# Fourth to eighth tile: the first product of mm2 is issued ahead of mm1's last two block products

## The chip, the cores and the metric

One NeuronCore of a Trainium2 chip runs the kernel. It has five engines, each with its own instruction queue worked through in order: TensorE (PE, matrix products; its weight loads are shown apart, as PEld), VectorE (DVE), ScalarE (ACT), GpSimd (POOL) and SyncE (SP), which here issues almost all the DMAs. The metric is the device time of one execution in microseconds. Three timed runs of the kernel before gave 269.88, 270.17 and 270.53 us; the median is 270.17 us.

## What is computed

Chunked attention over 8 batches of 576 tokens with 8 heads of 64, then a two-layer network with exact GELU over all 4608 tokens. The reference, cut:

```python
# attention inside chunks of 64 keys
scores = scale * np.matmul(q_c, k_c.transpose(0, 1, 2, 4, 3))
attn = np.exp(scores - max) / sum
x = np.matmul(attn, v_c)                # then 4608 x 512
# network: w_in is 512 x 2048, w_out is 2048 x 512
h = x @ w_in
g = 0.5 * h * (1.0 + erf(h * inv_sqrt2))
return g @ w_out
```

## The kernel before

**Tiles.** There are nine tiles of 512 tokens: for each batch its first 512 tokens, and a ninth tile with the last 64 tokens of all eight. For each tile the kernel runs `mm1` (x times w_in, then GELU into `h`, bf16) and `mm2` (`h` times w_out, stored as `y`). The attention of the next tiles is slipped between the products of `mm2`. The schedule is the program's own: every engine takes its instructions in the order in which the Python emits them, and a semaphore wait is put in wherever one reads or overwrites what another has not finished.

**Seven products.** From the fourth tile on (t = 3 to 8) both layers use a Winograd form of the 2 x 2 block product: seven block products in place of eight, with sums of blocks formed by VectorE and running sums kept in PSUM banks. In `mm1` the 2048 features are cut into four groups a, b, c, d. A group's products are numbered 1 to 7, each of them four matmuls (`prod`, L677). Products 1 and 2 go to a bank X, 7 and 4 to a bank Z, and 6, 5 and 3 to a bank Y that starts as a copy of product 1.

**The order by words.** `mm1_groups` (L646) reads its order from a string, `FOUR` (L639) for the tiles of this change. "3b" is product 3 of group b. "c1a" is the ACT copy of X into Y (L714), "c2a" the ACT copy and "c3a" the DVE copy of Y's running sum into SBUF (L725), "a1a" and "a2a" are the DVE additions of Z to these (L728). "g12d" is the GELU on ACT (L684) of group d, first feature half, second token half; "g21d" has the second feature half and the first token half. "h1", "h2", "h3" are the DVE sums of blocks of `h` (`h_sums`, L576 and L577) over two, four and two of the eight feature blocks. The tail of `FOUR` is

```
2c g11d 5d a1c 7d c3d 3c g21b 4c g11c 3b a1d
g22c 4d g12c g12b 3d a2c a2d g21c g22d g12d g21d h2 h3
```

**mm2.** `mm2_seven` (L761) runs seven products of sixteen matmuls each. Here they are named in their order before:

1. the first product, bank X (L781), copied by ACT into bank Y (L782); then the attention of the next tile, called by `also(1)`: the activation table for Exp, `rows_av` (64 small matmuls, L347) and `rows_x` (DVE, L362 and L363, with two DMA transposes on SP, L366)
2. the S2 product, added to Y (L787), which ACT then copies to `s2` (L788)
3. the second product, added to X (L789); ACT copies it to `y` (L790), and SP stores that quarter of the output (L791, issued in L857)
4. the S1 product, added to the same Y (L792), copied by ACT to `s5` (L793)
5. the T4 product in bank Z (L796), with the scores of a later tile (`quad_S`, L247) in its middle
6. the S3 product in bank W (L800)
7. the S4 product, added to Y (L805)

The banks of `mm1`'s Y and those of `mm2` (X, Y, Z, W) come in turn from one pool of three, `ps_mm`. A bank that is taken again waits for the last reader of its earlier use. The ninth tile has its own `mm2`, `last_seven` (L810).

Of the kernel before, what the change touches and what calls it, by code (L numbers as in the profile page):

```python
# [11 lines left out]
def kernel(  # L12
# [10 lines left out]
    P = 128  # L23
    f32 = mybir.dt.float32
# [547 lines left out]
    def h_sums(t, j0, j1):  # L572

        a11, a12, a21, a22 = h_blocks(t, j0, j1)
        s1, s2 = h_sum(t, 1, j0, j1), h_sum(t, 2, j0, j1)
        nc.vector.tensor_tensor(s1, a21, a22, op=mybir.AluOpType.add)  # L576
        nc.vector.tensor_tensor(s2, s1, a11, op=mybir.AluOpType.subtract)  # L577
# [37 lines left out]
    def x_sums(t, which=(1, 3, 2, 4)):  # L615
# [7 lines left out]
        for i in which:  # L623
# [16 lines left out]
               g12a c1d 2b a2a g22b 6d 5c g21a a2b 2d 7c h1 g11b c3c c2d 2c g11d 5d a1c 7d c3d 3c g21b 4c g11c 3b a1d  # L640
               g22c 4d g12c g12b 3d a2c a2d g21c g22d g12d g21d h2 h3"""

    FOURS = range(FIRST7, NT)
    PROGRAMS = {1: LATE, 2: THIRD, **{t: FOUR for t in FOURS}}

    def mm1_groups(t, extra, between={}):  # L646

        st = tiles[t]
        st["h"] = hpool.tile([P, FF, MT], bf16, tag="h", name="h")
        h = st["h"][:].rearrange("p f (m e) -> p f m e", m=2)  # L650
        b11, b12, b21, b22 = x_blocks(t)
        w = in_blocks()
        TT, add = nc.vector.tensor_tensor, mybir.AluOpType.add
        banks, sums = {}, {}
        four = t in FOURS
        tags = {"a": ("y_1", "y_2"), "b": ("y_5", "rc" if four else "y_2"), "d": ("y_1", "rc")}
        first = {"a": 0, "b": 4, "c": 2, "d": 6}
        plain = [] if four else [j + FH * r for j in (6, 7) for r in range(2)]
        hs = {"h1": (0, 2), "h2": (2, 6), "h3": (6, 8)}

        def prod(g, n):
            q, e = first[g] // 4, first[g] % 4
            if n in (1, 2):
                lhs, rhs, name = w[:, n - 1, :, 0, q, e:e + 2], b11 if n == 1 else b21, "X"
            elif n == 3:
                lhs, rhs, name = w_s[g, 4], b22, "Y"
            elif n == 4:
                lhs, rhs, name = w[:, 1, :, 1, q, e:e + 2], st["T"][4], "Z"
            else:
                lhs, rhs, name = w_s[g, n - 4], st["T"][n - 4], "Z" if n == 7 else "Y"  # L670
            fresh = n in (1, 7)
            if fresh:
                pool, tag = (ps_tp, "tp") if four and name == "Z" else (ps_at, "at")
                banks[g + name] = pool.tile([P, 2, TH], f32, tag=tag, name=f"h_{name}")
            for i in range(2):
                for kk in range(2):
                    nc.tensor.matmul(banks[g + name][:, i], lhs[:, kk, i], rhs[:, kk], start=fresh and i == kk == 0,  # L677
                                     stop=(kk == 1), skip_group_check=True)

        def gelu(g, r, m):  # L680
            j = first[g] + FH * r
            src = {(0, 0): lambda: banks[g + "X"], (0, 1): lambda: banks[g + "Y"],
                   (1, 0): lambda: sums[g, 0], (1, 1): lambda: sums[g, 1]}[r, m]()
            nc.scalar.activation(h[:, j:j + 2, m], src[:], Act.Gelu)  # L684

        for word in PROGRAMS.get(t, PROGRAM).split():
            for u in extra.pop(word, ()):
                u()
            if word == "start":
                begun = mm1_slot(t, [plain.pop(0) for _ in range(4)], between, 1)  # L690
            elif word == "sums":
                x_sums(t)
            elif word == "p" and t == 1:
                begun.pop()()
            elif word == "p":
                f = plain.pop(0)
                bank = ps_tp.tile([P, MT], f32, tag="tp", name="h_ps")
                for ks in range(KS):
                    nc.tensor.matmul(bank[:].rearrange("p (s e) -> p s e", s=2), w_in_sb[:, ks, f * P:(f + 1) * P],  # L699
                                     by_halves(t)[:, :, ks] if t >= FIRSTX else  # L700
                                     st["x"][:, ks, :].rearrange("p (s e) -> p s e", s=2),
                                     start=(ks == 0), stop=(ks == KS - 1))
                nc.scalar.activation(st["h"][:, f, :], bank[:], Act.Gelu)
            elif word in hs:
                if t >= FIRST7:
                    h_sums(t, *hs[word])
            elif word[0].isdigit():
                prod(word[1], int(word[0]))
            elif word[0] == "g":
                gelu(word[3], int(word[1]) - 1, int(word[2]) - 1)  # L710
            elif word[:2] == "c1":
                g = word[2]
                banks[g + "Y"] = ps_mm.tile([P, 2, TH], f32, tag="mm", name="h_Y")
                AC(banks[g + "Y"][:], banks[g + "X"][:])  # L714
            elif word[:2] in ("c2", "c3"):
                g, i = word[2], int(word[1]) - 2
                if g != "c":
                    tag = tags[g][i]
                    sums[g, i] = work.tile([P, 2, TH], f32, tag=tag, name=f"h_{g}", bufs=2 if tag == "rc" else 1)
                elif i == 0:  # L720
                    pool, tag = (hsum, "s3") if t < B else (ypool, "y")
                    pair = pool.tile([P, 4, TH], f32, tag=tag, name="h_sb")
                    sums[g, 0] = pair[:, 0:2]
                    sums[g, 1] = pair[:, 2:4]
                (AC if i == 0 else DV)(sums[g, i][:], banks[g + "Y"][:])  # L725
            elif word[0] == "a":
                g, i = word[2], 2 - int(word[1])
                TT(sums[g, i][:], banks[g + "Z"][:], sums[g, i][:], op=add)  # L728
# [13 lines left out]
    def product(out, lhs, rhs, fresh, behind=lambda m: None, ms=range(TH // P)):  # L742

        for m in ms:
            for f in range(FH):
                nc.tensor.matmul(out[m], lhs[:, f, m * P:(m + 1) * P], rhs[:, f, :],  # L746
                                 start=fresh and f == 0 and (m == 0 or len(out) == 3), stop=(f == FH - 1),
                                 skip_group_check=True)
            behind(m)
# [8 lines left out]
    def halves(bank):  # L758
        return [bank[:, 0], bank[:, 1]]

    def mm2_seven(t, at={}):  # L761

        def also(i):
            for u in at.get(i, ()):
                u()
        st = tiles[t]
        h = st["h"][:].rearrange("p (k f) (m e) -> p k f m e", k=2, m=2)
        w = w_out_sb[:].rearrange("p (k f) (n e) -> p k f n e", k=2, n=2)
        T = [None] + [w_t[i] for i in range(1, 5)]
        def bank_mm():  # L770
            return ps_mm.tile([P, 2, NH], f32, tag="mm", name="y_ps")
        X, Y = bank_mm(), bank_mm()
        s2, s5 = (work.tile([P, 2, NH], f32, tag=nm, name=nm, bufs=1) for nm in ("y_2", "y_5"))
        y = [ypool.tile([P, 2, d_model], f32, tag="y", name="y_sb") for _ in range(2)]
        TT, add = nc.vector.tensor_tensor, mybir.AluOpType.add
        if t == B:
            s1 = work.tile([P, 2, NH], f32, tag="y_1", name="y_1", bufs=1)
            last_seven(t, h, w, T, (X, Y, bank_mm()), (s1, s2, s5), y)
            return
        also(0)  # L780
        product(halves(X), h[:, 0, :, 0], w[:, 0, :, 0], True)  # L781
        AC(Y[:], X[:])  # L782
        Z = bank_mm()
        st["Z"] = Z[:].rearrange("p m n -> p (m n)")
        also(1)
        h_third(t)
        product_by_f(halves(Y), h_sum(t, 2), T[2])  # L787
        AC(s2[:], Y[:])  # L788
        product(halves(X), h[:, 1, :, 0], w[:, 1, :, 0], False)  # L789
        AC(y[0][:, :, :NH], X[:])  # L790
        store(t, 0, 0, y)  # L791
        product(halves(Y), h_sum(t, 1), T[1], False)  # L792
        AC(s5[:], Y[:])  # L793
        h_fourth(t)
        also(2)
        product(halves(Z), h[:, 1, :, 1], T[4], True, lambda m: also((2, m)))  # L796
        TT(s2[:], Z[:], s2[:], op=add)
        also(3)
        W = bank_mm()
        product(halves(W), h_sum(t, 3), T[3], True)  # L800
        TT(y[1][:, :, NH:], W[:], s5[:], op=add)
        TT(y[1][:, :, :NH], W[:], s2[:], op=add)
        store_whole(t, 1, y)
        also(4)
        product(halves(Y), h_sum(t, 4), w[:, 1, :, 1], False)  # L805
        AC(y[0][:, :, NH:], Y[:])
        store(t, 0, 1, y)
        also(5)
# [406 lines left out]
```

## Time and profile before

| | us |
|---|---|
| median of three timed runs | 270.17 |
| the profiled execution, whole | 270.41 |
| its span, first to last instruction | 268.6 |
| PE busy in the span | 259.6 (97%) |
| DVE busy | 202.1 (75%) |
| ACT busy | 187.1 (70%) |
| POOL busy | 77.0 (29%) |

The profile shows one execution. In the timeline each row has the start in us from the span's start, the length in us, the engine, the line of the kernel, the operation, output and inputs, and how many instructions are merged; a bracket at the end has the idle time of the engine ahead of it and what ended it. A matmul's row lasts longer than the time until the next matmul may start, since matmuls are pipelined: sixteen of 256 columns take 1.75 us from start to start of what follows, and the row shows 1.91. The fifth tile (t = 4) is the one followed below; its `mm2` begins at 147.05 us.

### The profile page before, as it was taken

How to read it: one execution, taken by the hardware profiler on the slowest of the kernel's cores; microseconds unless marked ns; L12 is line 12 of the kernel's file. 1: busy time of each engine (PE TensorE's matmuls, PEld its weight loads, DVE VectorE, ACT ScalarE, POOL GpSimd, SP SyncE). 2: the span in 40 equal slices, each digit the busy share in tenths (PEclk: the TensorE clock that was granted, in tenths of full speed). 3: DMA queues.
4: the chain of work that ended last, by engine and by line, in shares of the span. 5: the costliest groups of instructions: out<-in, count | busy, mean ns of one | idle time of the engine just before them, and what ended most of it. 6: DMA issues, size and time to landing. Idle time of an engine off the chain costs nothing.

```text
span 268.6 us, 7554 instructions
## 1 busy us (share of the span) xinstructions
PE 259.6 (97%) x3077; PEld 195.6 (73%) x3092; DVE 202.1 (75%) x372; ACT 187.1 (70%) x364; POOL 77.0 (29%) x130
## 2 busy tenths in 40 slices
PE   7989999999999999999999999999999999999993
PEld 3554454476548654888888888888888888888882
DVE  2565775989997879589569956995699769958961
ACT  3466756797767967897689669957995799239700
POOL 3735667361440061441044103500362030000000
PEclk9999999999999999999999999999999999999998
DMA  7999999997979959999899989988886760430005
GB/s 230 285 377 402 395 388 243 237 286 194 336 205 261 244 123 231 279 237 191 232 232 231 177 216 242 264 152 206 237 193 146 166 192 0 89 138 12 2 2 156
DMA packets 127075, 56.59 MB, mean 211 GB/s; under 512 B 103488, under 2 KB 120896, under 8 KB 127040
## 3 DMA queue, kind: packets, MB, share of 16 engines
q1 hardware_dynamic: 126592, 55.59, 79.4%
q10 hardware_dynamic: 448, 0.52, 0.7%
q8 instruction: 24, 0.39, 0.6%
q14 instruction: 11, 0.09, 0.1%
HBM read 36.70 MB, written 9.44 MB: 172 GB/s over the span
## 4 chain that ended last, share of the span: by engine, by line
PE 92%; ACT 2%; DVE 1%; DMA 1%; issue 1%; POOL 0%; SPq 0%; ACTq 0%; DVEq 0%; POOLq 0%
PE y_ps L746 24%; PE h_Y L677 15%; PE y_ps L866 12%; PE h_Z L677 10%; PE h_X L677 10%; PE h_ps L538 6%; PE y_ps L891 4%; PE y_ps L755 4%; PE s_ps L247 2%; PE h_ps L699 1%; DMA arrival<-in_k_dram 1%; PE tp L170 1%; ACT y_ps L782 1%; PE warm L958 1%; PE rc_ps L484 1%
## 5 line engine op out<-in xcount | busy, mean ns | idle before, releaser
L677 PEld LDWEIGHTS <-w_in_s 128*128 128x128 bf16 x480 | 46.8, 98 | 6.1
L677 PEld LDWEIGHTS <-w_in_sb 128*128 128x128 bf16 x360 | 35.1, 98 | 6.5
L677 PE MATMUL h_X<-x,w_in_sb 128*128 128x256 bf16 x240 | 33.7, 272 | 0.0
L677 PE MATMUL h_Y<-x_t,w_in_s 128*128 128x256 bf16 x240 | 32.7, 272 | 0.0
L866 PE MATMUL y_ps<-w_out_sb,h 128*128 128x512 bf16 x137 | 31.7, 379 | 0.9 <-issue 0.8
L746 PEld LDWEIGHTS <-h_s 128*128 128x128 bf16 x304 | 29.7, 98 | 3.6 <-issue 0.2
L746 PEld LDWEIGHTS <-h 128*128 128x128 bf16 x288 | 27.8, 98 | 3.4
L218 POOL CAST v_nat<-arrival 128x1024 bf16<-128x1024 f32 x14 | 14.8, 1061 | 48.4 <-DMA arrival<-in_v_dram 48.3
L164 POOL CAST q_nat<-arrival 128x512 bf16<-128x512 f32 x33 | 19.4, 627 | 28.2 <-DMA arrival<-in_q_dram 19.1
L164 POOL CAST k_nat<-arrival 128x512 bf16<-128x512 f32 x34 | 21.9, 678 | 14.0 <-DMA arrival<-in_k_dram 10.1
L746 PE MATMUL y_ps<-w_t,h_s 128*128 128x256 bf16 x208 | 24.8, 273 | 0.0
L866 PEld LDWEIGHTS <-h 128*128 128x128 bf16 x144 | 13.3, 98 | 15.0 <-issue 0.2
L746 PE MATMUL y_ps<-w_out_sb,h 128*128 128x256 bf16 x192 | 22.9, 273 | 0.0
L963 ACT ACT_TABLE_LOAD x16 | 20.5, 1283 | 1.0 <-PEq L1199 0.7
L684 ACT ACTIVATE h<-h_Y 128x512 bf16<-128x512 f32 x30 | 17.7, 595 | 2.4 <-PE h_Y L677 1.9
L714 ACT COPY h_Y<-h_X 128x512 f32<-128x512 f32 x30 | 17.0, 582 | 2.8 <-PE h_X L677 2.6
L684 ACT ACTIVATE h<-h_X 128x512 bf16<-128x512 f32 x30 | 17.8, 597 | 1.4 <-PE h_X L677 0.6
L677 PE MATMUL h_Z<-x_t,w_in_s 128*128 128x256 bf16 x120 | 18.0, 273 | 0.0
L677 PE MATMUL h_Y<-x,w_in_s 128*128 128x256 bf16 x120 | 17.7, 273 | 0.0
L677 PE MATMUL h_Z<-x_t,w_in_sb 128*128 128x256 bf16 x120 | 17.4, 272 | 0.0
L725 DVE COPY h_a<-h_Y 128x512 f32<-128x512 f32 x8 | 5.5, 692 | 14.1 <-PE h_Y L677 14.1
L254 ACT ACTIVATE pT<-s_ps 128x512 bf16<-128x512 f32 x28 | 14.5, 601 | 2.3 <-PE s_ps L247 2.3
(148 smaller groups left out, 489.4 us busy)
## 6 DMA issues: line engine op xcount, KB each, us to landing
arrival<-in_q_dram SPq DMA_DIRECT2D x7, 1024.0 KB
arrival<-in_k_dram SPq DMA_DIRECT2D x24, 256.0 KB
out_dram<-y_sb SPq DMA_DIRECT2D x23, 256.0 KB
arrival<-in_v_dram SPq DMA_DIRECT2D x20, 256.0 KB
arrival<-in_moe_w_out_dram SPq DMA_DIRECT2D x4, 1024.0 KB
arrival<-in_v_dram SPq DMA_DIRECT2D x30, 128.0 KB
out_dram<-y_sb SPq DMA_DIRECT2D x5, 512.0 KB
arrival<-in_moe_w_in_dram SPq DMA_DIRECT2D x4, 512.0 KB
```

The source lines that it names most:

```text
L164: copy(st[nm][:, g].rearrange("p j r d -> p r j d"), st[nm + "f"][:, 2 * g:2 * g + 2])
L218: copy(st["v"][:, part[0], part[1], :D], st["vf"][:, part[0], part[1]])
L254: nc.scalar.activation(pT[:].rearrange("p u (c j) -> p u c j", j=J), s_ps[g2][c][:].rearrange("p u (j c) -> p u c j", j=J), Act.Exp, scale ...
L538: nc.tensor.matmul(h_ps[a][:], w_in_sb[:, ks, f * P:(f + 1) * P], st["x"][:, ks, :], start=(ks == 0), stop=(ks == KS - 1))
L677: nc.tensor.matmul(banks[g + name][:, i], lhs[:, kk, i], rhs[:, kk], start=fresh and i == kk == 0, stop=(kk == 1), skip_group_check=True)
L684: nc.scalar.activation(h[:, j:j + 2, m], src[:], Act.Gelu)
L714: AC(banks[g + "Y"][:], banks[g + "X"][:])
L746: nc.tensor.matmul(out[m], lhs[:, f, m * P:(m + 1) * P], rhs[:, f, :], start=fresh and f == 0 and (m == 0 or len(out) == 3), stop=(f == FH ...
L755: nc.tensor.matmul(out[m], lhs[:, f, m * P:(m + 1) * P], rhs[:, f, :], start=False, stop=(f == FH - 1), skip_group_check=True)
L866: nc.tensor.matmul(y_ps[:], st["h"][:, f, ms * P:(ms + 1) * P], w_out_sb[:, f, :], start=(f == 0), stop=(f == FF - 1))
L891: nc.tensor.matmul(tiles[t]["y_ps", ms][:], tiles[t]["h"][:, f, ms * P:(ms + 1) * P], w_out_sb[:, f, :], start=(f == 0), stop=False)
L963: nc.scalar.activation(act_scratch[:], rest[:, 0:1], func)
```

## The change

Tiles t = 3 to 7 take their order in `mm1` from a new string, `AHEAD`; the ninth keeps `FOUR`. In `AHEAD` two words are new: "X" issues the first product of `mm2`, and "cX" takes bank Y and issues its ACT copy. "X" stands behind 4c and ahead of 4d and 3d. 3b has moved from behind 4c to ahead of 3c, "h2" stands ahead of a2d, and some GELUs have changed places. `mm2` then begins with the second product, by feature blocks (`product_by_f`, both token halves of a block in turn), its copy and its store; `also(1)`, the S2 product and its copy follow, and behind these at once the S1 product.

```diff
+    AHEAD = """begin 1a 1b c1a 1c 6a 7a c1b c2a 6b 5a 2a c1c 6c c2b 5b 7b c3a g11a a1a c3b c2c 3a a1b 1d 4a g22a 4b
+               g12a c1d 2b a2a g22b 6d 5c g21a a2b 2d 7c h1 g11b c3c c2d 2c g11d 5d a1c 7d c3d 3b g21b g11c 3c a1d
+               g22c 4c g12b X g12c a2c 4d g22d g21c cX h2 a2d 3d g12d g21d h3"""
...
-    PROGRAMS = {1: LATE, 2: THIRD, **{t: FOUR for t in FOURS}}
+    PROGRAMS = {1: LATE, 2: THIRD, **{t: AHEAD if t < B else FOUR for t in FOURS}}
...
+            elif word == "X":
+                mm2_first(t)
+            elif word == "cX":
+                st["Y"] = bank_mm()
+                AC(st["Y"][:], st["X"][:])
...
+    def mm2_first(t):
+        h, w = out_blocks(t)
+        tiles[t]["X"] = bank_mm()
+        product(halves(tiles[t]["X"]), h[:, 0, :, 0], w[:, 0, :, 0], True)
+
     def mm2_seven(t, at={}):
...
-        X, Y = bank_mm(), bank_mm()
+        X, Y = (st["X"], st["Y"]) if t < B else (bank_mm(), bank_mm())
...
-        also(0)
-        product(halves(X), h[:, 0, :, 0], w[:, 0, :, 0], True)
-        AC(Y[:], X[:])
         Z = bank_mm()
         st["Z"] = Z[:].rearrange("p m n -> p (m n)")
+        product_by_f(halves(X), h[:, 1, :, 0], w[:, 1, :, 0])
+        AC(y[0][:, :, :NH], X[:])
+        store(t, 0, 0, y)
         also(1)
         h_third(t)
         product_by_f(halves(Y), h_sum(t, 2), T[2])
         AC(s2[:], Y[:])
-        product(halves(X), h[:, 1, :, 0], w[:, 1, :, 0], False)
-        AC(y[0][:, :, :NH], X[:])
-        store(t, 0, 0, y)
         product(halves(Y), h_sum(t, 1), T[1], False)
         AC(s5[:], Y[:])
```

`bank_mm` and `out_blocks` hold what stood inside `mm2_seven` before (a bank of `ps_mm`; the blocks of `h` and w_out).

More of the change, by code (lines that the diff above doesn't have):

```diff
@@ L759, in halves, with bank_mm, out_blocks @@
         return [bank[:, 0], bank[:, 1]]
+    def bank_mm():
+        return ps_mm.tile([P, 2, NH], f32, tag="mm", name="y_ps")
+    def out_blocks(t):
+        return (tiles[t]["h"][:].rearrange("p (k f) (m e) -> p k f m e", k=2, m=2),
+                w_out_sb[:].rearrange("p (k f) (n e) -> p k f n e", k=2, n=2))
+    def mm2_first(t):
+        h, w = out_blocks(t)
+        tiles[t]["X"] = bank_mm()
+        product(halves(tiles[t]["X"]), h[:, 0, :, 0], w[:, 0, :, 0], True)
     def mm2_seven(t, at={}):
@@ L766, in mm2_seven @@
         st = tiles[t]
-        h = st["h"][:].rearrange("p (k f) (m e) -> p k f m e", k=2, m=2)
-        w = w_out_sb[:].rearrange("p (k f) (n e) -> p k f n e", k=2, n=2)
+        h, w = out_blocks(t)
         T = [None] + [w_t[i] for i in range(1, 5)]
-        def bank_mm():
-            return ps_mm.tile([P, 2, NH], f32, tag="mm", name="y_ps")
-        X, Y = bank_mm(), bank_mm()
+        X, Y = (st["X"], st["Y"]) if t < B else (bank_mm(), bank_mm())
         s2, s5 = (work.tile([P, 2, NH], f32, tag=nm, name=nm, bufs=1) for nm in ("y_2", "y_5"))
```

## The prediction

> **What bounds the kernel now.** I read the busy time by stretches first, one stretch per tile from the start of its mm1 to the start of the next one's, then the timeline of the fifth tile (t = 4), engine by engine. Columns of the stretches: us, busy time of PE, PEld, DVE, ACT and POOL with their instructions, granted clock, DMA share, GB/s.
>
> ```profile
> 134.66:160.93 26.27, 26.22 (x355) 23.06 (x353) 20.19 (x40) 20.68 (x37) 7.05 (x12) 1.00 1.02 211
> 187.19:213.53 26.34, 26.29 (x354) 22.96 (x352) 21.43 (x40) 20.68 (x37) 8.34 (x14) 1.00 0.75 183
> ```
>
> PE is busy for 26.22 of 26.27 us and its clock is full. ACT (20.68) and DVE (20.19) have about six us to spare. So TensorE's own queue sets the time: whatever holds it back is added to the end, and little can be won. The seventh tile (second row) takes 0.07 us longer, and its DVE is busier by 1.24 us.
>
> PE over the change, fifth tile:
>
> ```profile
> 145.68 0.60 PE L677 MATMUL h_Y<-x,w_in_s 128*128 128x256 bf16 x4
> 146.18 0.60 PE L677 MATMUL h_Z<-x_t,w_in_sb 128*128 128x256 bf16 x4
> 146.61 0.60 PE L677 MATMUL h_Y<-x,w_in_s 128*128 128x256 bf16 x4
> 147.05 1.91 PE L746 MATMUL y_ps<-w_out_sb,h 128*128 128x256 bf16 x16
> 148.89 0.60 PE L347 MATMUL av_ps<-v_nat,pT 64*64 64x65 bf16 x50
> ...
> 149.67 1.91 PE L755 MATMUL y_ps<-w_t,h_s 128*128 128x256 bf16 x16
> 151.42 1.91 PE L746 MATMUL y_ps<-w_out_sb,h 128*128 128x256 bf16 x16
> 153.16 1.91 PE L746 MATMUL y_ps<-w_t,h_s 128*128 128x256 bf16 x16
> ```
>
> These are 3b, 4d, 3d, the first product, the attention's 64 small matmuls, the S2, second and S1 products. Sixteen matmuls take 151.42 - 149.67 = 1.75 us from start to start, so four take 0.437. 4d comes 0.06 late (0.50 behind 3b). The first product's sixteen are issued by 148.80; the small ones start 0.09 behind that.
>
> ACT and DVE in the same stretch:
>
> ```profile
> 145.44 0.60 ACT L684 ACTIVATE h<-h_Y 128x512 bf16<-128x512 f32 x1
> 146.32 0.60 ACT L684 ACTIVATE h<-h_Y 128x512 bf16<-128x512 f32 x1 [0.28 <-PE h_Y L677]
> 146.81 0.62 ACT L684 ACTIVATE h<-h_sb 128x512 bf16<-128x512 f32 x1
> 147.33 0.62 ACT L684 ACTIVATE h<-h_d 128x512 bf16<-128x512 f32 x1
> 147.85 0.59 ACT L684 ACTIVATE h<-h_Y 128x512 bf16<-128x512 f32 x1
> 148.33 0.63 ACT L684 ACTIVATE h<-h_d 128x512 bf16<-128x512 f32 x1
> 149.05 0.57 ACT L782 COPY y_ps<-y_ps 128x512 f32<-128x512 f32 x1
> 149.64 1.28 ACT L963 ACT_TABLE_LOAD   x1
> 150.93 0.20 ACT L963 ACTIVATE act_scratch<-rest 128x1 f32<-128x1 bf16 x1
> 151.67 0.59 ACT L788 COPY y<-y_ps 128x512 f32<-128x512 f32 x1 [0.54 <-PE y_ps L755]
> ```
>
> ```profile
> 145.43 0.69 DVE L728 TENSOR_TENSOR h_d<-h_Z,h_d 128x512 f32<-128x512 f32 x1
> 146.04 0.68 DVE L728 TENSOR_TENSOR h_sb<-h_Z,h_sb 128x512 f32<-128x512 f32 x1
> 146.81 0.69 DVE L728 TENSOR_TENSOR h_d<-h_Z,h_d 128x512 f32<-128x512 f32 x1
> 147.42 0.68 DVE L576 TENSOR_TENSOR h_s<-h 128x1024 bf16<-128x1024 bf16 x1
> 148.14 0.69 DVE L577 TENSOR_TENSOR h_s<-h_s,h 128x1024 bf16<-128x1024 bf16 x1
> 148.75 0.42 DVE L576 TENSOR_TENSOR h_s<-h 128x512 bf16<-128x512 bf16 x1
> 149.20 0.43 DVE L577 TENSOR_TENSOR h_s<-h_s,h 128x512 bf16<-128x512 bf16 x1
> 149.54 0.19 DVE L362 RECIPROCAL one<-av_ps 128x6 f32<-128x6 f32 x1
> ```
>
> ACT's rows from the top are g12c, g12b, g21c, g22d, g12d, g21d, the copy into Y, the Exp table, the copy to `s2`; DVE's are a1d, a2c, a2d, h2 (two), h3 (two), then `rows_x`. The late 4d is explained: a1d, which reads the bank that 4d adds to, ends at 146.12. And the S2 product starts at 149.67, 0.05 behind the end (149.62) of ACT's copy into Y, which began 2.00 behind the first product's start.
>
> **Gain one: the copy into Y.** How long the small matmuls would hold PE without that copy is seen at the 64 of `quad_S` in the fourth tile, which wait for nothing:
>
> ```profile
> 128.74 0.74 PE L247 MATMUL s_ps<-q_t,k_t 64*64 64x64 bf16 x64
> 129.41 0.83 PE L746 MATMUL y_ps<-w_t,h 128*128 128x256 bf16 x6
> ```
>
> 0.67 us, against 149.67 - 148.89 = 0.78. After the change the copy lies a whole product ahead, under 4d and 3d, so 0.11 a tile is gained. **Gain two:** 4d stands behind X and no longer meets a1d: 0.06.
>
> **The tail of mm1, new order** (fifth tile). 3b, 3c and 4c take the slots of 3c, 4c and 3b, so 4c starts at 145.68. X at 146.12, 4d at 147.86, 3d at 148.30, the second product at 148.74. X's bank was group b's Y; its last reader g12b starts at 145.44 (3b in 3c's slot gives it what g12c got) and ends at 146.04, 0.08 ahead of X. If it came later each 0.1 would be paid; I take nothing. cX starts 2.00 behind X, at 148.12, and ends at 148.69, in time for 148.74, with nothing to spare. The second product's last quarter, its thirteenth step, due at 148.74 + 12 x 0.109 = 150.05, reads what g21d writes. g21d needs a2d, which needs 4d: a2d started 0.63 behind 4d before, so 148.49, and ends at 149.18. h2, moved ahead of a2d on DVE's queue, starts behind a2c (4c + 0.63 = 146.31, + 0.61 = 146.92), and ends at 148.33, under X, so it costs nothing here. g12d starts 0.64 behind 3d (as g12b behind 3b before), 148.94; g21d 0.48 behind that, 149.42, ending 150.05. With 0.05 for the release and the 0.1 of a weight load the step starts about 0.15 late. Bounds: 0, if release and load hide; 0.36 where DVE is slow, as in the seventh tile:
>
> ```profile
> 199.95 1.05 DVE L576 TENSOR_TENSOR h_s<-h 128x1024 bf16<-128x1024 bf16 x1
> 201.04 0.98 DVE L577 TENSOR_TENSOR h_s<-h_s,h 128x1024 bf16<-128x1024 bf16 x1
> ```
>
> There h2 ends 52.53 + 146.92 + 2.07 = 201.52 by the same steps (52.53 is two tiles, 187.19 - 134.66), half a us behind 4d's results at 201.02, so a2d and g21d come 0.21 later. The 0.07 that this tile now loses goes: its h3, late today, is done ahead of the S2 product.
>
> **The loss: the copy to s2 has no cover left.** The S2 and S1 products add to the same bank Y, and between them ACT must read Y (L788). Today the second product lies there, 1.75 us, over a copy that ends at 151.67 + 0.59 = 152.26, 0.90 before PE asks for Y at 153.16. After the change the S1 product follows the S2 product directly and, PE's queue being in order, all behind it waits too. From the S2 product's start: 2.00 to the copy's, 0.59, 0.05 to release: 2.64 in place of 1.75, so **0.89 a tile**. That PE does wait in this place is seen in the ninth tile, where VectorE reads Y between the same two products and only half a product lies between:
>
> ```profile
> 254.03 1.91 PE L746 MATMUL y_ps<-w_t,h_s 128*128 128x256 bf16 x16
> ...
> 256.05 0.69 DVE L821 TENSOR_TENSOR y<-y_ps,y 128x512 f32<-128x512 f32 x1 [0.73 <-PE y_ps L746]
> ...
> 256.79 0.93 PE L746 MATMUL y_ps<-w_t,h_s 128*128 128x256 bf16 x7
> ```
>
> Start to read 2.02, read 0.69, release 0.05: 2.76 in all, the same three terms. Bounds for the copy: 0.87 (with the 0.57 of the copy into Y) to 1.01 (with this 0.69 and 2.02).
>
> Is ACT free for it? The second product ends about 150.8, its copy at 151.4; table and dummy take 1.49 and end at 152.9. The S2 product starts at 148.74 + 1.75 + 0.15 + 0.09 + 0.67 = 151.40, so the copy is due at 153.40: 0.5 to spare.
>
> The Trainium skill, ScalarE: Activation LUTs, What ACT_TABLE_LOAD costs, gives a switch of tables about 1283 ns for the load and another 1380 for a drain. The trace agrees with the first and shows no second: the load starts 0.02 behind the copy ahead of it, and the dummy 0.01 behind the load. By the page the copy to `s2` would be some 0.9 later in the four tiles that load Exp, an estimate of 3.6 us more.
>
> **What else moves.** The attention of the next tile starts at 150.73 in place of 148.89. `rows_x` waited for h3 on DVE until 149.54; it now waits for PE's small matmuls, some 0.5 behind their start (an estimate: the first bank is full after 24 of the 64, 0.25, and the last of these must end, 0.2), so it is 1.7 later, and so are its two transposes:
>
> ```profile
> 151.63 3.50 SPq L366 DMA_TRANSPOSE x<-x_r  x2
> ```
>
> They were issued by 155.13, 5.8 ahead of the next mm1 at 160.93; that mm1 is itself 0.87 later, so 5.0 is left. I take nothing. The store of the first quarter moves ahead of them on SP; the copy it waits for ends at 151.4, before the rows are ready, so no one queues behind it. Loads behind the transposes on SP shift with the tile. POOL's queue is untouched. h3 ends 149.54 + 0.9 = 150.4, ahead of the S2 product.
>
> **Sum, against the profiled execution's own 270.41.** A tile: - 0.11 - 0.06 + 0.15 + 0.89 = 0.87. Four such tiles 3.48; the seventh 0.87 + 0.21 - 0.07 = 1.01. Together + 4.5: 274.9. The profiled run lies 0.24 above the median of 270.17, so **274.7** for a median.
>
> **Rivals.** (1) *The read of Y is not waited for.* If the S1 product were let into Y while ACT reads it, or behind its first half, the 0.89 would go and a tile would come out at - 0.02, or - 0.17 if the tail's 0.15 goes too: 270.2 to 269.3, not slower. It decides as soon as under 0.02 of the 0.89 is left. For it speaks nothing but that both products only add; against it the ninth tile's 256.79 and the S2 product's 149.67, each 0.05 behind the end of a read. 3 in 100.
> (2) *The tail of mm1 becomes the bound.* DVE's h2 ahead of a2d at the seventh tile's speed everywhere gives 4 x 0.21 = 0.8 more, 275.5; with X also held by g12b by 0.1 a tile, 276.0. For it: cX and g12b with under 0.1 to spare. Against: one tile in five shows the slow sums. 10 in 100.
> (3) *The Exp table pushes the copy to s2.* If ACT needed another 1.28 behind each load, the copy would start at 154.2, 0.8 later, in t = 3 to 6: + 3.2, 277.9. The rows put 0.01 there. 2 in 100. The rule named above is what would make it so.
> (4) *The tail is free*: g21d in time everywhere, the copy at its lower bound: five tiles at 0.70 and the seventh's 0.07, + 3.4, 273.6. 15 in 100.
>
> **How the numbers follow.** The forecast has 70 in 100. The range goes down to (4) less the 0.3 by which the three runs differ from their median, 273.3, and up to the far end of (2), 276.0; it leaves out (1), (3) and what no case names, some 10 in 100. A measurement of this kernel tells 0.2% (0.54 us) from no change. Faster by that: 0.02, the better half of (1); within: 0.02; slower: 0.96.
>
> **What would show it.** Right: between the S2 and S1 products' starts 2.64 in five tiles, L788 in it; the S2 product 0.67 behind the small matmuls' start; 4d with no gap; a wait of 0.1 to 0.4 inside the second product, ended by ACT's GELU; tiles of 27.1 us in place of 26.27. Wrong: 1.75 between those two starts, gaps at X's first matmul, the copy starting behind the dummy of the table, or PE waiting for `x` at the next mm1.

## The result and the profile after

The changed kernel takes 274.21 us (median of 6 runs, 273.61 to 274.69), against 270.35 for the kernel before (6 runs, 269.56 to 271.37). The ratio is 1.0141, with a 95% interval from 1.0116 to 1.0167: slower, by 3.9 us. The profiled execution took 274.16 us, its span 272.4.

The same stretches as before, mm1 to mm1, of the fifth and the seventh tile of the changed kernel (us; PE, PEld, DVE, ACT, POOL busy; clock; DMA share; GB/s):

```profile
135.31:162.38 27.07, 26.34 (x355) 22.91 (x353) 20.34 (x40) 20.78 (x37) 7.21 (x12) 1.00 0.97 206
189.44:216.51 27.07, 26.34 (x355) 22.89 (x353) 20.84 (x40) 20.77 (x37) 7.85 (x14) 1.00 0.83 186
```

The fifth tile takes 0.80 us more than before (26.27), and of the 27.07 PE is now idle for 0.73. The clock is still full. PE's timeline shows where:

```profile
146.33 0.60 PE L681 MATMUL h_Z<-x_t,w_in_sb 128*128 128x256 bf16 x4
146.76 1.91 PE L755 MATMUL y_ps<-w_out_sb,h 128*128 128x256 bf16 x16
148.51 0.60 PE L681 MATMUL h_Z<-x_t,w_in_sb 128*128 128x256 bf16 x4
148.95 0.60 PE L681 MATMUL h_Y<-x,w_in_s 128*128 128x256 bf16 x4
149.39 1.98 PE L764 MATMUL y_ps<-w_out_sb,h 128*128 128x256 bf16 x16
151.30 0.60 PE L347 MATMUL av_ps<-v_nat,pT 64*64 64x65 bf16 x50
...
151.97 1.92 PE L764 MATMUL y_ps<-w_t,h_s 128*128 128x256 bf16 x16
154.62 1.91 PE L755 MATMUL y_ps<-w_t,h_s 128*128 128x256 bf16 x16 [0.73 <-ACT y L806]
```

The rows are 4c, X (the first product), 4d, 3d, the second product, the small matmuls of the attention, the S2 and the S1 product. From 4c to the second product each one follows the last without a gap. From S2 to S1 it is 2.65 us in place of 1.75, and the bracket at S1 names what ended the 0.73 of idle time: ACT's copy to `s2`, L806 here. ACT in the same stretch:

```profile
148.77 0.57 ACT L715 COPY y_ps<-y_ps 128x512 f32<-128x512 f32 x1 [0.45 <-PE y_ps L755]
149.58 0.60 ACT L688 ACTIVATE h<-h_Y 128x512 bf16<-128x512 f32 x1 [0.25 <-PE h_Y L681]
150.08 0.62 ACT L688 ACTIVATE h<-h_d 128x512 bf16<-128x512 f32 x1
151.40 0.58 ACT L801 COPY y_sb<-y_ps 128x512 f32<-128x512 f32 x1 [0.70 <-PE y_ps L764]
152.00 1.28 ACT L978 ACT_TABLE_LOAD   x1
153.30 0.20 ACT L978 ACTIVATE act_scratch<-rest 128x1 f32<-128x1 bf16 x1
153.98 0.59 ACT L806 COPY y<-y_ps 128x512 f32<-128x512 f32 x1 [0.48 <-PE y_ps L764]
```

ACT idles 0.48 ahead of the copy, waiting for the S2 product: the copy is neither late nor long, but PE has nothing else to do while it runs. The list of waits sums it up (who waited for whom: us in total, times, longest):

```profile
PE y_ps L755 <- ACT y L806: 3.6, 5, 0.7
```

Five times 0.73, one for each changed tile. From start to start that is 0.89 each, since a product's last matmul runs on for 0.16 behind the next one's slot.

### The profile page after: what moved, and what is told of

Its sections match the earlier page's. It is cut to its first block, busy times and chain, and to the rows that moved or that the text cites. A ratio compares the mean times of both kernels' runs of the same rounds, so it can differ in the third digit from the quotient of the medians.

```text
span 272.4 us, 7553 instructions
## 1 busy us (share of the span) xinstructions
PE 259.1 (95%) x3077; PEld 194.2 (71%) x3092; DVE 202.6 (74%) x372; ACT 187.7 (69%) x364; POOL 78.0 (29%) x130
## 4 chain that ended last, share of the span: by engine, by line
PE 89%; SPq 4%; DMA 2%; ACT 1%; issue 1%; POOL 0%; DVE 0%; ACTq 0%
PE y_ps L755 21%; PE h_Y L681 15%; PE y_ps L881 11%; PE h_Z L681 10%; PE h_X L681 10%; PE y_ps L764 7%; PE h_ps L538 5%; PE y_ps L906 4%; DMA arrival<-in_moe_w_in_dram 2%; SPq L149 2%; PE s_ps L247 2%; SPq L108 1%; PE h_ps L703 1%; ACT y L806 1%; PE av_ps L347 1%
## 5 line engine op out<-in xcount | busy, mean ns | idle before, releaser
L218 POOL CAST v_nat<-arrival 128x1024 bf16<-128x1024 f32 x14 | 15.5, 1114 | 47.6 <-DMA arrival<-in_v_dram 47.5
L881 PEld LDWEIGHTS <-h 128*128 128x128 bf16 x144 | 13.4, 98 | 15.0 <-issue 0.2
L755 PEld LDWEIGHTS <-h 128*128 128x128 bf16 x208 | 20.0, 98 | 2.4
L681 PE MATMUL h_Y<-x,w_in_s 128*128 128x256 bf16 x120 | 16.9, 273 | 0.0
L538 PE MATMUL h_ps<-x,w_in_sb 128*128 128x512 bf16 x67 | 15.1, 379 | 0.1
```

The source lines that it names most:

```text
L218: copy(st["v"][:, part[0], part[1], :D], st["vf"][:, part[0], part[1]])
L538: nc.tensor.matmul(h_ps[a][:], w_in_sb[:, ks, f * P:(f + 1) * P], st["x"][:, ks, :], start=(ks == 0), stop=(ks == KS - 1))
L881: nc.tensor.matmul(y_ps[:], st["h"][:, f, ms * P:(ms + 1) * P], w_out_sb[:, f, :], start=(f == 0), stop=(f == FF - 1))
```

## The experiments

Theory A: the loss is ACT's read of Y, left without cover between S2 and S1. Rivals: R1, mm1's new order; R2, the later attention. The tiles' times come from the profiles, one execution each, and are the sharper measure, since the time until the fourth tile's mm1 begins, where these kernels are still alike, lay between 107.9 and 110.2 us in different profiles. "Five tiles" is the time from the start of the fourth tile's mm1 to that of the ninth's: 130.62 us before, 134.53 in the changed kernel. Each ratio is taken to runs of the kernel before that were made beside that kernel's own: their median is 270.35 us for the changed kernel, 271.15 for the second form with S3, and 270.43 for the others.

| kernel | five tiles | median us | ratio to before, interval |
|---|---|---|---|
| before | 130.62 | 270.35 | |
| changed | 134.53 | 274.21 | 1.0141, 1.0116 to 1.0167 |
| swap only | 134.97 | 274.74 | 1.0158, 1.0120 to 1.0197 |
| second product back as cover | 131.48 | 271.83 | 1.0056, 1.0024 to 1.0087 |
| s2 read from another bank | 131.37 | 271.36 | 1.0026, 0.9999 to 1.0053 |
| read twice | 137.74 | 279.33, one run | |
| second product by halves | 137.81 | 277.87, one run | |
| attention as cover | 139.60 | 278.89, one run | |
| h2 behind a2d | 134.58 | 274.84, one run | |
| S3 as cover | 130.90 | 271.36 | 1.0044, 1.0014 to 1.0073 |
| S3 as cover, second form | 131.31 | 271.40 | 1.0003, 0.9968 to 1.0037 |
| S3 as cover, third form | 130.88 | 271.60 | 1.0036, 1.0009 to 1.0063 |

**Swap only.** The kernel before, with the second product ahead of S2 and nothing else changed:

```diff
+        product(halves(X), h[:, 1, :, 0], w[:, 1, :, 0], False)
+        AC(y[0][:, :, :NH], X[:])
+        store(t, 0, 0, y)
         h_third(t)
         product_by_f(halves(Y), h_sum(t, 2), T[2])
         AC(s2[:], Y[:])
-        product(halves(X), h[:, 1, :, 0], w[:, 1, :, 0], False)
-        AC(y[0][:, :, :NH], X[:])
-        store(t, 0, 0, y)
         product(halves(Y), h_sum(t, 1), T[1], False)
```

> The kernel before with one thing changed: in mm2 of t = 3 to 7 the second product, its copy and its store stand ahead of the S2 product, behind the attention; mm1's order and the first product's place are as before. Theory A: PE waits 0.89 ahead of S1 in five tiles, tile 27.16, whole 270.35 + 4.45 = 274.8. R1 (mm1's new order costs) and R2 (the later attention costs): neither is in this kernel, so 26.27 a tile and 270.4.

The fourth to seventh tile take 27.14 to 27.15 us, the whole 274.74. PE, fifth tile (second, S2, S1):

```profile
150.61 1.91 PE L746 MATMUL y_ps<-w_out_sb,h 128*128 128x256 bf16 x16
152.36 1.91 PE L755 MATMUL y_ps<-w_t,h_s 128*128 128x256 bf16 x16
155.00 1.25 PE L746 MATMUL y_ps<-w_t,h_s 128*128 128x256 bf16 x10 [0.73 <-ACT y L791]
```

S2 to S1 is 2.64, with the same 0.73 of idle time and the same kind of releaser. With mm1's order and the attention's place untouched, the swap alone gives 4.35 us in the five tiles. So neither R1 nor R2 is needed for the loss.

**Second product back as cover.** The changed kernel, with that product between S2 and S1 again:

```diff
-        product_by_f(halves(X), h[:, 1, :, 0], w[:, 1, :, 0])
-        AC(y[0][:, :, :NH], X[:])
-        store(t, 0, 0, y)
         also(1)
         h_third(t)
         product_by_f(halves(Y), h_sum(t, 2), T[2])
         AC(s2[:], Y[:])
+        product_by_f(halves(X), h[:, 1, :, 0], w[:, 1, :, 0])
+        AC(y[0][:, :, :NH], X[:])
+        store(t, 0, 0, y)
```

> The changed kernel with the second product back between the S2 and S1 products; the first product stays ahead of 4d and 3d, and the attention follows 3d at once. Theory A (the loss is ACT's read of Y with no cover between S2 and S1, 0.89 a tile): S1 starts 3.49 behind S2 with no wait; the gain of 0.06 at 4d stays; the small matmuls now wait some 0.3 for the bank that g12d reads last, so the tile takes about 26.4 us (27.07 in the changed kernel, 26.27 before) and the whole about 271.0 (270.2 to 271.6). Rival R1 (the cost lies in mm1's new order): tile 27.0 to 27.1, whole 274.2. Rival R2 (the cost lies in the later attention): also near 271, but then without any wait ahead of S1 having been there.

The fourth to seventh tile take 26.42 to 26.53, the five 131.48: the wait at S1 is gone, the one at 4d too. S2 (149.56) to S1 (153.06) has two full products:

```profile
148.56 0.82 PE L347 MATMUL av_ps<-v_nat,pT 64*64 64x65 bf16 x50
...
149.56 1.92 PE L764 MATMUL y_ps<-w_t,h_s 128*128 128x256 bf16 x16
151.32 1.91 PE L764 MATMUL y_ps<-w_out_sb,h 128*128 128x256 bf16 x16
```

The small matmuls now take 1.00 to S2 in place of 0.67, because they stand directly behind 3d and meet two banks that are still being read, one by a2d on DVE and one by a GELU on ACT:

```profile
148.23 0.69 DVE L737 TENSOR_TENSOR h_d<-h_Z,h_d 128x512 f32<-128x512 f32 x1 [0.26 <-PE h_Z L681]
```

```profile
148.66 0.60 ACT L688 ACTIVATE h<-h_Y 128x512 bf16<-128x512 f32 x1 [0.25 <-PE h_Y L681]
```

These end at 148.92 and 149.26; the small matmuls stop twice, for 0.22 until 148.98 and for 0.11 until 149.31. So X's early place costs a third of a us there, and takes more than it won. As the source of the 0.8 a tile R1 falls. The median of the whole, 271.83, lies above the 270.2 to 271.6 that was expected. The profiled execution, to which the tiles belong, took 270.67; where the longer ones lost more is not shown.

**s2 read from another bank.** ACT's copy to `s2` reads X, so the part of the output that is formed with `s2` has another value:

```diff
-        AC(s2[:], Y[:])
+        AC(s2[:], X[:])
```

> The changed kernel with ACT's copy to s2 taken from bank X in place of bank Y, so that S1 needn't wait for it; the half of the output that is formed with s2 gets another value. All else, mm1's order and the place of the attention included, is the changed kernel's. Theory A: no wait ahead of S1, tile 27.07 - 0.89 = 26.17, whole 274.2 - 4.45 = 269.8, a little under the kernel before. R1 and R2: 27.07 and 274.2.

The fourth tile does as A says (26.16), the other four don't: 26.51 to 26.52 and, for the eighth, 25.67; the whole is 271.36 where 269.8 was expected. PE of the fifth tile (S2, S1, T4), and what DVE does ahead of T4:

```profile
152.01 1.92 PE L764 MATMUL y_ps<-w_t,h_s 128*128 128x256 bf16 x16
153.77 1.91 PE L755 MATMUL y_ps<-w_t,h_s 128*128 128x256 bf16 x16
155.79 1.03 PE L755 MATMUL y_ps<-w_t,h 128*128 128x256 bf16 x8
```

```profile
155.31 0.42 DVE L363 TENSOR_TENSOR x_r<-y_ps,one 128x256 bf16<-128x256 f32 x1
```

S1 no longer waits (1.76 behind S2). But T4, due at 155.52, starts at 155.79, 0.06 behind the end of the last of `rows_x`, which reads bank Z (`y_ps` in the row). The attention is later in the changed kernel, and this is where that would be paid; there S1's wait lies over it. In the fourth tile `quad_S` stands ahead of T4, 0.67 of other work, and T4 does not wait. So R2 is a second wait behind the first, not part of the loss. It accounts for 0.27 of the 0.35 that the fifth tile takes more than the fourth; the rest, 0.08, is a gap in the scores behind it.

**Attention as cover.** To see that second wait alone, the small matmuls were put between S2 and S1:

```diff
-        also(1)
-        h_third(t)
         product_by_f(halves(Y), h_sum(t, 2), T[2])
         AC(s2[:], Y[:])
+        also(1)
+        h_third(t)
         product(halves(Y), h_sum(t, 1), T[1], False)
```

> The changed kernel with the attention of the next tile moved behind the S2 product, so that the 64 small matmuls stand between S2 and S1 as cover. By theory A alone: 0.76 of the 0.89 is covered, S2 to S1 2.65 with 0.12 of waiting, tile 26.3. But the run without the read of Y showed a second wait behind the first, T4's for bank Z, which the x rows on DVE still read (0.27 there): here these rows start some 1.8 later, so T4 should wait about 1.9 and the tile take 28.1; whole 279. If that second wait was something else (the other copies on ACT): 26.3 and 270.5.

The fifth to seventh tile take 28.26 (the fourth 27.40), the whole 278.89, where 28.1 and 279 were expected. T4 waits, and the bracket names the reader:

```profile
157.00 0.42 DVE L363 TENSOR_TENSOR x_r<-y_ps,one 128x256 bf16<-128x256 f32 x1
157.34 1.21 DVE L581 TENSOR_TENSOR h_s<-h 128x2048 bf16<-128x2048 bf16 x1
157.47 1.03 PE L755 MATMUL y_ps<-w_t,h 128*128 128x256 bf16 x8 [1.75 <-DVE x_r L363]
```

**Read twice.**

```diff
         AC(s2[:], Y[:])
+        AC(s2[:], Y[:])
```

> The changed kernel with the copy to s2 issued twice, one behind the other. Theory A (PE waits for the end of ACT's last read of Y): the second copy starts some 0.5 behind the first and S1 another 0.5 later: S2 to S1 3.14 in place of 2.65, tiles 27.56, whole 274.2 + 2.5 = 276.7. If the wait were a fixed price of adding twice to one bank: 2.65 and 274.2.

```profile
156.52 0.58 ACT L806 COPY y<-y_ps 128x512 f32<-128x512 f32 x1 [0.47 <-PE y_ps L764]
...
157.13 0.58 ACT L807 COPY y<-y_ps 128x512 f32<-128x512 f32 x1
157.77 0.49 PE L755 MATMUL y_ps<-w_t,h_s 128*128 128x256 bf16 x3 [1.34 <-ACT y L807]
```

S1 starts 0.06 behind the end of the second copy, 0.62 later than with one: PE waits for the end of the last read of Y, so it is not a fixed price of adding twice to one bank. The step was expected at 0.5, but these two copies do not overlap (0.61 from start to start). Five tiles 137.74, 3.2 more than the changed kernel. The single run's 279.33 has another 2 us in it, from ahead of the fourth tile's mm1 (110.2 against 108.3).

**Second product by halves.**

```diff
-        product_by_f(halves(X), h[:, 1, :, 0], w[:, 1, :, 0])
+        product(halves(X), h[:, 1, :, 0], w[:, 1, :, 0], False)
```

> The changed kernel with the second product by token halves in place of feature blocks, so that its seventh step, not its thirteenth, is the first to need g21d. Theory: the wait of 0.06 inside the second product becomes 0.06 + 6 x 0.109 = 0.72, but S1's wait doesn't change; tiles 27.73, whole 277.4. If ACT's GELU isn't what that wait is for: 27.07 and 274.2.

```profile
150.45 0.82 PE L755 MATMUL y_ps<-w_out_sb,h 128*128 128x256 bf16 x6
151.82 1.27 PE L755 MATMUL y_ps<-w_out_sb,h 128*128 128x256 bf16 x10 [0.55 <-ACT h L688]
```

The seventh step starts 1.37 behind the first, where six steps take 0.655: 0.72 of waiting for the GELU, as forecast, and 27.71 to 27.72 for the fourth to seventh tile. The order by feature blocks hides all but 0.06 of it.

**h2 behind a2d.**

```diff
-g22c 4c g12b X g12c a2c 4d g22d g21c cX h2 a2d 3d g12d g21d h3
+g22c 4c g12b X g12c a2c 4d g22d g21c cX a2d h2 3d g12d g21d h3
```

> The changed kernel with h2 on DVE behind a2d in place of ahead of it. The prediction's step (h2 ahead of a2d costs nothing, being under X): the wait inside the second product stays 0.06 and S1's wait 0.89. But h2 and h3 then run some 1.4 us later on DVE, and the x rows behind them; their last read of bank Z ends about 157.1 on the fifth tile's clock, where T4 wants the bank at 156.4: T4 waits 0.8, tile 27.8 to 27.9, whole 278. If the place of h2 doesn't matter: 27.07 and 274.2.

The time did not change: 27.06 a tile, 134.58 in five. The prediction's reading of h2 holds (it costs nothing ahead of a2d), but the expectation for T4 was wrong: DVE had idle time behind a2d, h2 and h3 ran through it, and `rows_x` came only 0.15 later, which the wait at S1 still covers.

**S3 as cover.** The S3 product has a bank of its own, so it can lie over the read:

```diff
-        also(1)
         h_third(t)
+        also(1)
         product_by_f(halves(Y), h_sum(t, 2), T[2])
         AC(s2[:], Y[:])
+        W = bank_mm()
+        product(halves(W), h_sum(t, 3), T[3], True)
         product(halves(Y), h_sum(t, 1), T[1], False)
...
```

The cut part moves the y additions accordingly and `quad_S` ahead of T4.

> The changed kernel with the S3 product (bank W) moved between S2 and S1 as cover; DVE forms its h sum ahead of the next tile's x rows, the scores of a later tile stand ahead of the T4 product. Theory A: the read of Y lies under 1.75 us of S3, no wait ahead of S1, tile 26.17, whole 269.8, 0.5 under the kernel before, if the moved DVE sum and the later x rows cost nothing. If x or the scores come late: 0.2 to 0.6 a tile back, 270.8 to 272.8. R1 and R2: 274 or more.

The stretches of the fourth to seventh tile:

```profile
108.95:135.12 26.17, 26.17 (x354) 22.88 (x353) 19.76 (x37) 20.38 (x37) 6.86 (x11) 1.00 0.95 228
135.12:161.57 26.45, 26.34 (x355) 22.86 (x353) 20.87 (x40) 20.57 (x37) 7.38 (x12) 1.00 0.98 221
161.57:187.74 26.17, 26.17 (x354) 22.86 (x352) 20.36 (x40) 20.68 (x37) 5.76 (x10) 1.00 0.94 212
187.74:214.27 26.53, 26.26 (x354) 22.86 (x352) 20.89 (x39) 20.66 (x38) 7.44 (x14) 1.00 0.88 187
```

Two tiles reach 26.17, a tenth under the kernel before, and the wait at S1 is gone in all. The others lose it again: the fifth 0.28 at X, which waits for g12b, and the seventh 0.35 at 4b, which waits for the DVE addition a1b. The second form moved the scores behind S3, the sums of x ahead of the last y addition, and h1 behind a1c with what hangs on it on POOL:

> The changed kernel with S3 as cover between S2 and S1, as in the earlier run with S3 there, and three places mended where that run lost time: the later tile's scores stand right behind S3, the sums h1 on DVE behind a1c (POOL's casts that follow h1 with them), the sums of the next tile's x ahead of the second of the y additions. Theory: no wait ahead of S1, none at X; tiles 26.17 (t = 3 to 6) and 25.39 (t = 7), 130.1 in the five against 130.6 before; whole 269.9, about 0.2% under the kernel before. If x, the DVE sums under POOL's casts or ACT's queue come late in single tiles as they did there: 26.2 to 26.5 and 270.2 to 271.4.

The third put h1 back:

> The last version (S3 as cover, scores behind S3, x sums ahead of the second y addition) with h1 and what hangs on it on POOL back in the changed kernel's place. Theory: the waits that the last version met in the fourth tile (a2d behind an h2 slowed by POOL's casts, 0.33) and the seventh (scores waiting for a late key transpose, 0.82) came from POOL's casts starting 2 us later, so they go; what may stay is 0.28 at X in the fifth tile. Tiles of t = 3 to 7 together 130.1 to 130.6 (130.62 before, 131.31 in the last version), whole within 0.2% of the kernel before, 269.8 to 270.9. If those waits have another source: 131 or more in the five tiles.

The second form lost 0.33 in the fourth tile and 0.82 at the scores in the seventh; the third has three tiles of 26.16, but 26.72 and 25.68 in the last two, where 4b waits 0.34, the scores 0.20 and, in the eighth, X 0.30. So its 130.88 misses the 130.1 to 130.6 that was expected. By their medians all three come out between equal to the kernel before and 0.4% slower. None is shown to beat it. The third form is slower by about 1 us, for 0.26 of which the five tiles account. In its profiled execution another 0.84 lies ahead of the fourth tile's mm1, which begins at 109.24 in place of 108.40; why is left open.

## Why the prediction was right

**The loss at S1** was forecast at 0.89 a tile from the fifth tile's rows before, with the ninth tile's as a like case, and is 0.89 in each of five tiles. The swap alone shows the cause, the double read its size.

**The gains** came as worked out: the S2 product starts 0.67 behind the small matmuls (0.78 before), and 4d 1.75 behind X, with no gap. X met no wait in any of the five tiles, and cX ended at 149.34 for a second product at 149.39: as tight as forecast. That X cost nothing is partly luck. g12b ended 0.07 ahead of it, and a release takes 0.05; with the same order of mm1, X waited 0.10 for g12b in the fifth tile with the second product back as cover, and 0.28 with S3 as cover.

**The table load** begins 0.02 behind the copy ahead of it and the dummy ends 0.48 ahead of the copy to `s2`; 0.5 was forecast. The rival with a second wait behind the load got nothing.

**The term that was mis-sized** is the wait inside the second product: 0.15 a tile, measured 0.06. PE's weight loads there:

```profile
149.28 1.30 PEld L764 LDWEIGHTS <-h 128*128 128x128 bf16 x12
150.75 0.33 PEld L764 LDWEIGHTS <-h 128*128 128x128 bf16 x4 [0.17 <-ACT h L688]
```

g21d ends at 150.70, to the hundredth where it was worked out relative to the slots. The thirteenth load starts 0.05 behind that, and the whole product's row is 1.98 long in place of 1.91. The 0.05 for the release was right; the 0.1 of a weight load was not paid on top. With this term the whole came out between the forecast of 274.7 and the 273.6 of rival (4), whose tail costs nothing.

**The seventh tile's extra 0.21 did not come.** It was taken over from one slow pair of DVE sums, as if it belonged to the tile. It belongs to POOL's casts: before, these began at 199.85, with h2 at 199.95; in the changed kernel they begin at 202.56, when h2's second sum is already under way. That sum keeps its 0.69, and the casts lie over h3, which has slack:

```profile
201.71 0.68 DVE L576 TENSOR_TENSOR h_s<-h 128x1024 bf16<-128x1024 bf16 x1
202.42 0.69 DVE L577 TENSOR_TENSOR h_s<-h_s,h 128x1024 bf16<-128x1024 bf16 x1
203.28 0.69 DVE L737 TENSOR_TENSOR h_d<-h_Z,h_d 128x512 f32<-128x512 f32 x1 [0.17 <-PE h_Z L681]
204.34 0.63 DVE L576 TENSOR_TENSOR h_s<-h 128x512 bf16<-128x512 bf16 x1 [0.38 <-ACT h L688]
```

```profile
202.56 2.88 POOL L164 CAST k_nat<-arrival 128x512 bf16<-128x512 f32 x4 [2.02 <-issue]
```

So the five tiles took 3.9 more in place of 4.5: the two terms, 0.09 a tile and 0.21 once, account for the difference to within 0.1. Rival (2), the tail of mm1 as the bound, did not show in the changed kernel, though its mechanism exists: in the second form with S3 as cover, POOL's casts met h2 in the fourth tile and cost 0.33 there.

**What was not seen**: that the later attention had a second wait ready at T4. It was looked for at the next tile's x only, not at bank Z, which `rows_x` reads. It cost nothing here because it lay under the first.

## What to carry to other kernels

When a product is moved, ask what it was covering where it stood, not only what it gains where it goes: two products into one accumulator with a copy between them need something else on TensorE's queue until the copy has been read out and the bank released, here 0.89 us. A wait that is found and removed may have another right behind it that it covered, so price the second before counting on the whole of the first. And a slow row is not a property of its tile until it is known what ran beside it.

## What the runs showed of the hardware

DVE's bf16 sums of two SBUF operands take longer beside POOL's casts: in the kernel before, the sum over 1024 columns took 1.05 us at 199.95 and 0.68 in the fifth tile, and POOL's casts stood right over it.

```profile
199.85 3.39 POOL L164 CAST k_nat<-arrival 128x512 bf16<-128x512 f32 x4 [1.56 <-DMA arrival<-in_k_dram]
```

Here is the same pair over the fourth tile's h2 in the second form with S3:

```profile
121.71 0.90 DVE L576 TENSOR_TENSOR h_s<-h 128x1024 bf16<-128x1024 bf16 x1
122.65 0.98 DVE L577 TENSOR_TENSOR h_s<-h_s,h 128x1024 bf16<-128x1024 bf16 x1
123.55 0.68 DVE L737 TENSOR_TENSOR h_d<-h_Z,h_d 128x512 f32<-128x512 f32 x1
```

```profile
120.90 3.20 POOL L164 CAST k_nat<-arrival 128x512 bf16<-128x512 f32 x4 [4.68 <-DMA arrival<-in_k_dram]
```

The addition that reads one operand from PSUM keeps its 0.68. The Trainium skill, SBUF — State Buffer, Who interferes with whom, states this: a DVE instruction with two SBUF inputs contends with a GpSimd instruction that reads SBUF. The traces agree.

They also show how: the two take turns, and the one that begins second pays. The twelve profiles hold 144 of these sums over 1024 columns. Eighteen began while a cast was running, and each of them ended 0.54 to 0.55 us behind the end of that cast. Four began first and met a cast only later; they kept 0.68 to 0.69. In all twenty cases in which a cast began during a sum, the cast ended 0.47 behind the sum; the one at 202.56 in the changed kernel so took 1.02 in place of 0.61. No sum took over 0.70 without a cast that had begun before it. So the price hangs on which of the two comes a tenth of a us earlier. In both POOL rows of this section the bracket names the landing of a key's DMA as what the casts waited for, so the slow sums would move from tile to tile with the transfers' timing; that is likely but not shown, and for the changed kernel's row the profile names no such cause.
